# Banded attention and a ratio MLP on one core: where the attention probabilities are transposed

## Chip, cores and metric

One core of one Trainium2 chip runs the whole program. The metric is device time in microseconds, the median of several executions of the same program. Lower is better. The kernel before takes 993.1 us.

## What is computed

The reference is an attention over a causal band of 128 positions, followed by a two-layer MLP whose activation is a ratio of two polynomials:

```python
# batch 8, heads 8, sequence 576, head size 64
scores = scale * q @ k.T + bias           # bias: -slope[head] * distance
mask   = (rel >= 0) & (rel < 128)         # rel = query position - key position
attn   = exp(scores - max); attn = attn / (sum(attn) + 1e-09)
x      = attn @ v                         # as 4608 tokens x 512
h      = x @ w_in                         # 512 x 2048
P = a0 + a1*h + a2*h**2 + a3*h**3
Q = 1 + |b0|*|h| + |b1|*h**2
out    = (P / (Q + 1e-06)) @ w_out        # 2048 x 512
```

## The kernel before

The 4608 tokens are 36 blocks of 128. The MLP works on tiles of two blocks (256 tokens), 18 in all. For each tile, a step takes two chunks of 128 columns of the hidden layer: TensorE makes `h` (24 matmuls of 256 columns, three for each of four slices of the 512 inputs and each chunk, since every f32 factor is split in a high and a low part), the other engines work out the ratio on 128x512 elements, and TensorE adds the chunk to the output sums `acc` (12 matmuls of 512 columns). A tile has 8 steps, the program 144.

The elementwise chain of a step is a line of instructions on three engines, in `mlp`: ScalarE takes |h| (L959) and one linear term (L961), GpSimd makes the denominator (L960, L962), VectorE the numerator (L963, L964), ScalarE takes logarithm and exponential of the denominator (L965, L967), VectorE corrects the reciprocal and multiplies (L968, L969, L975), ScalarE rounds the high part `g_h` (L385), and VectorE subtracts to get the low part `g_l` (L977). `h` lies in a PSUM bank from its first matmul to L977. Three banks (tag `h`) serve `h` and the bank `px` of the attention.

The attention works in units: a pair of heads over two blocks, 76 units, 4 for each later tile. A unit's TensorE work is put into *sessions* between MLP matmuls (`attention`, L667). The session of unit u holds three things, one after the other:

- the transposes of unit u-1's probabilities (`turn_halves`, L593): eight transposes of 64x128 pieces against an identity, written to PSUM, half of them into `px` and half into free columns of the score banks,
- the scores of unit u (`scores`, L537),
- the product of probabilities and values of unit u-2 (`quarters`, L641), into `px` and `py`.

Between the sessions the unit's softmax runs: VectorE moves the upper half of each diagonal block (`copy_predicated`, L561) and adds bias and takes the minimum (L568, the tile `pr`), ScalarE exponentiates and sums (L573), VectorE takes the reciprocal (L584), GpSimd scales `pr` by it (L585, `shares`). After the transposes, ScalarE copies the results out of PSUM into `p_all` (`spread`, L607, three copies by the helper at L385), and GpSimd splits them by two affine selects into the part of the own block and the part of the block before (L619). `quarters` reads `p_all`. After it, `sum_halves` (L652) brings the result into the input `x` of the next tile's MLP.

The order of all instructions on each engine is not written by hand. `Plan.op` records every operation with a due time and a cost for each engine that may do it. `Plan.order` first places a fixed list (`FIRST`, L59), then runs a small model in time in which every free engine takes the ready operation that is due first, and the program is emitted in the order found. So the constants at L355 to L362 (due times) and the costs given to `plan.op` decide the order on every engine.

DMAs are issued by SyncE (SP): the queries, keys and values of a unit (`job`, L477, tiles `kq` and `v`, four buffers each), bias tables (L530) and the output (L1039).

```python
# L681, in attention(u): what a session is made of
emits = [lambda: c.scores(sc)]
if turned: emits.insert(0, lambda: turned.turn_halves(places))
if held:   emits.append(lambda: held["unit"].quarters(...))
```

Of the kernel before, what the change touches and what calls it, by code (L numbers as in the profile page):

```python
# [20 lines left out]
P = 128  # L21
# [318 lines left out]
def banded_attention_ratio_mlp(ctx: ExitStack, tc: tile.TileContext, kqv, w_in, w_out, ab, bias, ident, out):  # L340
# [21 lines left out]
    PAIRED, PA, PT, PD, TO, TL, EO, SO2 = 76, -0.35, 6.0, 3.0, 0.0, 0.1, 0.0, 0.0  # L362
# [145 lines left out]
    class Unit:  # L508

        def __init__(self, u, A):  # L510
            self.u, self.A = u, A
            self.t, self.p, self.j = t, p, j = units[u]
            self.m = m = TILES[j]
            self.n = 2 * m
            self.kinds = [block_type(STARTS[j] + i) for i in range(m)]
            self.blocks = [i for i in range(m) if self.kinds[i] != 1]
            self.kt, self.qt, self.vt, self.kq_keys, self.v_keys = job(u, A)
            self.tables, self.bias_keys = [], []
            for kind in self.kinds:
# [12 lines left out]

# [21 lines left out]
        def softmax(self, sc, heads=(0, 1), lead=0.0):  # L554
# [11 lines left out]
            def top(e, i, h):  # L566
                y = 2 * i + h
                nc.vector.tensor_tensor_reduce(  # L568
                    out=ap(pr)[:, y, :], in0=inside(sc[h])[:, i, Q:], in1=self.tables[i](h), scale=-0.125, scalar=3.0e38,
                    op0=ALU.add, op1=ALU.min, accum_out=ap(st)[:, y : y + 1])  # L570

            def exp(e, y):
                nc.scalar.activation(ap(pr)[:, y, :], ap(pr)[:, y, :], AF.Exp, bias=ap(st)[:, y : y + 1], scale=-1.0, accum_out=ap(st)[:, 4 + y : 5 + y])  # L573

            for i in range(m):
                for h in heads:
                    y = 2 * i + h
                    plan.op(A + 0.6 - lead, {"v": 211}, lambda e, i=i, h=h: top(e, i, h), reads=[(sc[h], 0), self.bias_keys[i]], writes=[(pr, y), (st, y)])
                    plan.op(A + 0.8, {"a": 388}, lambda e, y=y: exp(e, y), reads=[(pr, y), (st, y)], writes=[(pr, y), (st, 4 + y)])

        def shares(self):
# [3 lines left out]
            plan.op(A + 1.2, {"g": 185 + 1.6 * P * n}, lambda e: nc.gpsimd.tensor_tensor(ap(pr)[:, :n], ap(pr)[:, :n], ap(st)[:, 12 : 12 + n, None].to_broadcast([P, n, P]), ALU.mult),  # L585
# [81 lines left out]
    def attention(u):  # L667
# [20 lines left out]
        if held:  # L688
# [3 lines left out]
            writes += [(bank, 0), (held["py"], 0)]  # L692
        o1 = plan.op(A, {"p": cost}, lambda e: [x() for x in emits], reads=reads, writes=writes, rows=0.5)
# [10 lines left out]
        if late:  # L704
# [425 lines left out]
```

## Time and profile before

| | |
|---|---|
| median of 3 runs | 993.1 us (992.41 to 993.13) |
| the profiled execution | 995.22 us, of which 993.5 us are the span from first to last instruction |
| granted TensorE clock | 0.997 of full speed |
| busy: TensorE, VectorE, ScalarE, GpSimd | 99%, 77%, 70%, 55% |
| bytes moved by DMA | 69 MB |

In the profile PE is TensorE, PEld its weight loads, DVE is VectorE, ACT is ScalarE, POOL is GpSimd, SP is SyncE. A line such as L598 is line 598 of the kernel. Times are microseconds unless marked ns.

### The profile page before, as it was taken

The page shows a single profiled execution, that of the slowest core. Times are in us where ns is not written, and L with a number is a line of the kernel's source. Part 1 is how long each engine was busy: PE and PEld are TensorE (multiplying, and loading weights), DVE is VectorE, ACT ScalarE, POOL GpSimd, SP SyncE. Part 2 cuts the span into 40 slices and gives each one's busy share as a digit, 9 for nine tenths or more (in the row PEclk, how much of TensorE's full clock was granted, in tenths as well). Part 3 has the DMA queues.
Part 4 walks back from the last instruction along what each step waited for, and adds up shares of the span by engine and source line. Part 5 has one row for each costly group of instructions (what it writes and reads, how often), then busy time and mean ns, then how long its engine had stood idle before and what let it go on. Part 6 is the DMA issues. An engine that isn't in the chain of part 4 may idle for free.

```text
span 993.5 us, 24565 instructions
## 1 busy us (share of the span) xinstructions
PE 986.2 (99%) x9429; PEld 862.6 (87%) x9431; DVE 769.0 (77%) x1843; ACT 690.6 (70%) x1717; POOL 549.7 (55%) x662
## 2 busy tenths in 40 slices
PE   8999999999999999999999999999999999999998
PEld 5767888888989888898898898988899889898997
DVE  4999988877777877777777877777777777777675
ACT  5999776676767666767667767767666767766563
POOL 3799965555545554545564545455554545454332
PEclk8999999999999999999999999999999999999999
DMA  8973312111212111112111211111111111000000
GB/s 263 342 257 110 105 43 74 44 65 49 71 49 71 44 44 63 56 44 65 54 45 46 74 46 51 66 44 66 53 44 64 55 44 59 37 10 23 1 22 22
DMA packets 45140, 69.08 MB, mean 70 GB/s; under 512 B 4448, under 2 KB 29664, under 8 KB 45024
## 3 DMA queue, kind: packets, MB, share of 16 engines
q1 hardware_dynamic: 44736, 67.26, 20.3%
q8 instruction: 74, 1.21, 0.5%
q14 instruction: 42, 0.34, 0.1%
q10 hardware_dynamic: 288, 0.26, 0.1%
HBM read 58.07 MB, written 9.44 MB: 68 GB/s over the span
## 4 chain that ended last, share of the span: by engine, by line
PE 98%; DMA 1%; SPq 1%; DVE 0%; issue 0%; ACT 0%; ACTq 0%
PE h L931 42%; PE acc L995 42%; PE sc L552 6%; PE px L650 4%; PE px L598 2%; DMA kq<-in_kqv 1%; PE py L650 1%; PE px L742 1%; PE pt L591 0%; PE warm L1051 0%; PE h L937 0%; SPq L486 0%; SPq L844 0%; SPq L487 0%; PE sc L598 0%
## 5 line engine op out<-in xcount | busy, mean ns | idle before, releaser
L931 PE MATMUL h<-x_hi,wi_hi 128*128 128x256 f32 x1024 | 290.9, 284 | 0.0
L931 PE MATMUL h<-x_lo,wi_hi 128*128 128x256 f32 x1024 | 287.9, 281 | 0.0
L931 PE MATMUL h<-x_hi,w_lo 128*128 128x256 f32 x1024 | 287.5, 281 | 0.0
L960 POOL TENSOR_SCALAR g_q<-g_u,babs 128x512 f32<-128x512 f32 x142 | 110.1, 775 | 247.1 <-ACT g_u L959 243.1
L931 PEld LDWEIGHTS h<-x_lo,wi_hi 128*128 128x128 f32 x1024 | 192.6, 188 | 36.3
L995 PE MATMUL acc<-wo_hi,g_h 128*128 128x512 f32 x548 | 220.2, 402 | 0.0
L995 PE MATMUL acc<-w_lo,g_h 128*128 128x512 f32 x548 | 216.3, 395 | 0.0
L931 PEld LDWEIGHTS h<-x_hi,wi_hi 128*128 128x128 f32 x1024 | 193.1, 189 | 23.2 <-issue 1.4
L995 PE MATMUL acc<-wo_hi,g_l 128*128 128x512 f32 x548 | 206.7, 395 | 0.0
L931 PEld LDWEIGHTS h<-x_hi,w_lo 128*128 128x128 f32 x1024 | 193.7, 189 | 0.0
L962 POOL TENSOR_TENSOR g_q<-g_q,g_u 128x512 f32<-128x512 f32 x143 | 185.1, 1295 | 13.8 <-DVE g_q L960 2.9
L965 ACT ACTIVATE g_u<-g_q,guard 128x512 f32<-128x512 f32 x144 | 104.4, 725 | 103.7 <-POOL g_q L962 102.2
L963 DVE TENSOR_TENSOR g_p<-h,g_p 128x512 f32<-128x512 f32 x144 | 99.5, 691 | 90.4 <-ACT g_p L961 88.7
L968 DVE SCALAR_TENSOR_TENSOR g_q<-g_q,h 128x512 f32<-128x512 f32 x144 | 98.7, 685 | 68.3 <-ACT h L967 68.0
L959 ACT ACTIVATE g_u<-h 128x512 f32<-128x512 f32 x141 | 83.9, 595 | 95.8 <-PE h L931 95.7
L619 POOL TENSOR_SCALAR_AFFINE_SELECT p_all<-p_all 128x512 f32<-128x512 f32 (+1 forms) x144 | 90.6, 629 | 69.7 <-ACT p_all L385 61.7
L573 ACT ACTIVATE pr<-pr,st 128x128 f32<-128x128 f32 x288 | 114.7, 403 | 8.1 <-DVE st L568 7.8
L961 ACT ACTIVATE g_p<-h,na 128x512 f32<-128x512 f32 x140 | 108.7, 776 | 0.9 <-PE h L931 0.9
L977 DVE TENSOR_TENSOR g_l<-h,g_h 128x512 fp32r<-128x512 f32 x137 | 93.8, 685 | 19.9 <-ACT g_h L385 19.5
L995 PEld LDWEIGHTS acc<-wo_hi,g_h 128*128 128x128 f32 x548 | 103.2, 188 | 6.2 <-issue 0.7
L964 DVE SCALAR_TENSOR_TENSOR g_p<-g_p,na,h 128x512 f32<-128x512 f32 x144 | 106.8, 742 | 1.8
L969 DVE SCALAR_TENSOR_TENSOR h<-g_p,na,h 128x512 f32<-128x512 f32 x144 | 107.9, 749 | 0.0
(110 smaller groups left out, 1800.2 us busy)
## 6 DMA issues: line engine op xcount, KB each, us to landing
kq<-in_kqv SPq DMA_DIRECT2D x68, 320.0 KB, 3.2
v<-in_kqv SPq DMA_DIRECT2D x68, 192.0 KB, 2.4
out<-o SPq DMA_DIRECT2D x34, 256.0 KB, 2.0
raw_w<-in_w_in SPq DMA_DIRECT2D x16, 512.0 KB, 6.3
raw_w<-in_w_out SPq DMA_DIRECT2D x16, 512.0 KB, 5.2
bias_t<-in_bias SPq DMA_DIRECT2D x44, 64.0 KB, 2.9
kq<-in_kqv SPq DMA_DIRECT2D x4, 192.0 KB, 5.5
kq_first<-in_kqv SPq DMA_DIRECT2D x4, 128.0 KB, 3.0
```

What stands on the lines that cost most here:

```text
L573: nc.scalar.activation(ap(pr)[:, y, :], ap(pr)[:, y, :], AF.Exp, bias=ap(st)[:, y : y + 1], scale=-1.0, accum_out=ap(st)[:, 4 + y : 5 + y])
L931: nc.tensor.matmul(h(i), w[:, k, :], x[:, k, :], start=(k == 0 and m == 0), stop=(k == NKC - 1 and m == len(seq) - 1))
L960: plan.op(E, {"g": tsc, "v": dve(W / 2, 1)} if soon else {"g": tsc}, lambda e: eng[e].tensor_scalar(v(g_q), v(g_u), ap(babs)[:, 1:2], ap(b ...
L961: plan.op(E, either(soon, act(W, 1, 2) - 20, dve(W, 2)), lambda e: nc.scalar.activation(v(g_p), v(h_s), AF.Identity, bias=ap(na)[:, 2:3], ...
L962: plan.op(E, {"g": ttc, "v": dve(W)} if soon else {"g": ttc}, lambda e: eng[e].tensor_tensor(v(g_q), v(g_q), v(g_u), ALU.mult), reads=[(g_ ...
L963: plan.op(E, {"v": dve(W)}, lambda e: nc.vector.tensor_tensor(v(g_p), v(h_s), v(g_p), ALU.mult), reads=[(h_s, 0), (g_p, 0)], writes=[(g_p, ...
L964: plan.op(E, {"v": dve(W, 1)}, lambda e: stt(v(g_p), v(g_p), ap(na)[:, 1:2], v(h_s), ALU.add, ALU.mult), reads=[(h_s, 0), (g_p, 0)], write ...
L965: plan.op(E, {"a": act(W, 0, 1)}, lambda e: nc.scalar.activation(v(g_u), v(g_q), AF.Ln, bias=guard, scale=1.0), reads=[(g_q, 0)], writes=[ ...
L968: plan.op(E, {"v": dve(W)}, lambda e: stt(v(g_q), v(g_q), GUARD, v(h_s), ALU.add, ALU.mult), reads=[(g_q, 0), (h_s, 0)], writes=[(g_q, 0)])
L969: plan.op(E, {"v": dve(W, 1)}, lambda e: stt(v(h_s), v(g_p), ap(na)[:, 0:1], v(h_s), ALU.add, ALU.mult), reads=[(g_p, 0), (h_s, 0)], write ...
L977: plan.op(E, {"v": dve(W)}, lambda e: nc.vector.tensor_tensor(v(g_l), v(h_s), v(g_h).bitcast(F32), ALU.subtract), reads=[(h_s, 0), (g_h, 0 ...
L995: nc.tensor.matmul(ap(accs[n][i]), x[:, sl], w, start=(c == c0 and part == 0 and m == 0), stop=(c == c1 - 1 and (part == 1 or plain) and m ...
```

## The change

From unit 24 to unit 73 (50 units, the four of each tile from the sixth on, without the last two units) the transpose no longer runs on TensorE. VectorE transposes the 16 blocks of 32x32 of each 128x128 matrix where they are, into a tile `z`. `z` is stored to HBM (256 KB), and four loads of 64 KB bring each block to its place in the tile `x_turn`. GpSimd's two affine selects then read `x_turn` in place of `p_all`. For this the columns of `pr` are laid out in four groups of 32 for each of the four matrices, so softmax, scaling and `quarters` address pieces of 32 columns. The three ScalarE copies out of PSUM are gone for these units. `z` and `x_turn` alternate between two buffers each, in memory that earlier parts of the program have left. Some due times of the planner are changed too, and one entry of `FIRST` follows the new numbering.

```diff
-    1294, 1359, 1276, 1369, 1354, 11372, 1319, 1320, 1356, 1373, 1350, 1714, 1376, 1321, 1250, 1322, 1226, 1295, 1297, 1299, 1357, 1277,
+    1294, 1359, 1276, 1369, 1354, 11372, 1319, 1320, 1356, 1373, 1350, 1722, 1376, 1321, 1250, 1322, 1226, 1295, 1297, 1299, 1357, 1277,
...
-    SA, SG, LL, ML, ZA, ME = 0.082, 0, 6.123, 22.844, 0.779, -17.957
+    SA, SG, LL, ML, ZA, ME = 0.082, 0, 6.123, 19.678, 0.779, -17.272
...
-    SL, AW, BL, E0, E1, E2 = -9.614, 22.396, 14.524, 24.893, 13.935, 57.569
+    SL, AW, BL, E0, E1, E2 = -9.614, 22.396, 18.599, 24.893, 13.935, 57.569
...
+    CROSS, CT, CM = 24, 2.27, 0.744
...
+            self.y = (lambda i, h: m * h + i) if self.crossed() else (lambda i, h: 2 * i + h)
...
+        def crossed(self):
+            return CROSS <= self.u < len(units) - 2
...
+        def row(self, y):
+            if not self.crossed():
+                return ap(self.pr)[:, y, :]
+            return ap(self.pr).rearrange("q y c -> q (y c)").rearrange("q (k y c) -> q k y c", y=4, c=32)[:, :, y]
...
+        def cross(self):
+            u, A, m, n, pr = self.u, self.A, self.m, self.n, self.pr
+            z = slot(const, [P, 4, n, 32], F32, "z", tag=("spare0", "part")[u % 2])
+            d = slot(dr4, [P, 4, n, 32], F32, "z_dram")
+            x = slot(const, [P, 4, n, 32], F32, "x_turn", tag=("raw", "w1")[u % 2])
+            w = self.w = slot(sb2, [P, 2, 4 * n, 32], F32, "p_all")
...
+            plan.op(A + CT, {"s": 728}, lambda e: eng[e].dma_start(ap(d), ap(z)), reads=[(z, 0)], writes=[(d, 0)])
+            for k in range(4):
+                r = slice(32 * k, 32 * k + 32)
+                plan.op(A + CT, {"s": 182}, lambda e, k=k, r=r: eng[e].dma_start(ap(x)[r], ap(d)[:, k].rearrange("(g a) y c -> a g (y c)", a=32)), reads=[(d, 0)], writes=[(x, k)])
+            cost = {"g": 135 + 0.93 * n * P}
...
+        if u > CROSS and not turned:
+            cost += 70
...
-        if late:
+        if c.crossed():
+            c.cross()
+        elif late:
             turning.append(c)
```

On TensorE this is one session of the steady part. Before, with the transposes (L598) ahead of the scores (L552) and the value products (L650):

```order
L995 MATMUL acc_8206<-wo_hi,g_l 128x512
L598 MATMUL px<-id_sb,pr 128x64
L598 MATMUL sc_8286<-id_sb,pr 128x64
...
L598 MATMUL px<-id_sb,pr 128x64
L598 MATMUL sc_8291<-id_sb,pr 128x64
L552 MATMUL sc_8286<-kq 64x2x64
L552 MATMUL sc_8291<-kq 64x2x64
...
L650 MATMUL px<-p_all,v 64x128 x2
L650 MATMUL py<-p_all,v 64x128 x2
```

And a session of the change (L558 are the scores, L694 the value products):

```order
L1044 MATMUL acc_8142<-wo_hi,g_l 128x512
L558 MATMUL sc_8421<-kq 64x2x64
L558 MATMUL sc_8423<-kq 64x2x64
...
L694 MATMUL px<-p_all,v 64x128 x2
L694 MATMUL py<-p_all,v 64x128 x2
```

The eight transposes are gone and scores follow the MLP matmul directly; TensorE has 6545 rows where it had 6945. The number of MLP matmuls between sessions changed as well: before, a tile's four sessions stand behind 33 `h` and 14 `acc` matmuls, 39 and 22, 33 and 14, 87 and 46; now behind 48 and 24, 21 and 14, 51 and 22, 72 and 36.

On VectorE the new transpose (L629) stands between the instructions of the MLP's elementwise chain. Before, the chain of one step near there:

```order
L968 SCALAR_TENSOR_TENSOR g_q_8543<-g_q_8543,h_8411 128x512
L969 SCALAR_TENSOR_TENSOR h_8411<-g_p_8541,na_489,h_8411 128x512
L975 SCALAR_TENSOR_TENSOR h_8411<-g_q_8543,h_8411 128x512
L963 TENSOR_TENSOR g_p_8636<-h_8537,g_p_8636 128x512
L977 TENSOR_TENSOR g_l_8644<-h_8411,g_h_8640 128x512
```

Now, in the same part of a step (L1017, L1018, L1024 and L1026 are the old L968, L969, L975 and L977, L1012 the old L963):

```order
L1017 SCALAR_TENSOR_TENSOR g_q_8605<-g_q_8605,h_8481 128x512
L629 STREAM_TRANSPOSE z_8662<-pr_8602 128x512
L1018 SCALAR_TENSOR_TENSOR h_8481<-g_p_8597,na_491,h_8481 128x512
L1012 TENSOR_TENSOR g_p_8668<-h_8583,g_p_8668 128x512
L1024 SCALAR_TENSOR_TENSOR h_8481<-g_q_8605,h_8481 128x512
L1013 SCALAR_TENSOR_TENSOR g_p_8668<-g_p_8668,na_491,h_8583 128x512
L1026 TENSOR_TENSOR g_l_8704<-h_8481,g_h_8697 128x512
```

Of the 50 transposes 11 stand like this one inside a step's last VectorE instructions; 35 stand right behind an L1026, at the end of a step's chain, and of these 10 have the next session's L567 (the old L561) behind them.

On GpSimd the affine selects stood behind the MLP pair (L960, L962) after the session that made the transposes. Before:

```order
L585 TENSOR_TENSOR pr_8371<-pr_8371,st_8372 128x512
L960 TENSOR_SCALAR g_q_8432<-g_u_8423,babs_495 128x512
L962 TENSOR_TENSOR g_q_8432<-g_q_8432,g_u_8423 128x512
L619 AFFINE_SELECT p_all_8489<-p_all_8489 128x4x128 x2
L960 TENSOR_SCALAR g_q_8543<-g_u_8530,babs_495 128x512
```

Now, where `pr_8499` is the scaling of the unit whose selects write `p_all_8701`:

```order
L621 TENSOR_TENSOR pr_8499<-pr_8499,st_8500 128x512
L1009 TENSOR_SCALAR g_q_8605<-g_u_8590,babs_497 128x512
L1011 TENSOR_TENSOR g_q_8605<-g_q_8605,g_u_8590 128x512
L621 TENSOR_TENSOR pr_8602<-pr_8602,st_8603 128x512
L1009 TENSOR_SCALAR g_q_8676<-g_u_8664,babs_497 128x512
L1011 TENSOR_TENSOR g_q_8676<-g_q_8676,g_u_8664 128x512
L636 AFFINE_SELECT p_all_8701<-x_turn_8636 128x512 x2
L1009 TENSOR_SCALAR g_q_8764<-g_u_8760,babs_497 128x512
```

Two MLP pairs and the next unit's scaling now stand between a unit's scaling and its selects.

## Rows read from the trace of the kernel before

**Rows 1.** The page: busy time by engine, and the chain that ended last.

```profile
PE 986.2 (99%) x9429; PEld 862.6 (87%) x9431; DVE 769.0 (77%) x1843; ACT 690.6 (70%) x1717; POOL 549.7 (55%) x662
...
PE 98%; DMA 1%; SPq 1%; DVE 0%; issue 0%; ACT 0%; ACTq 0%
PE h L931 42%; PE acc L995 42%; PE sc L552 6%; PE px L650 4%; PE px L598 2%; DMA kq<-in_kqv 1%; PE py L650 1%; PE px L742 1%; PE pt L591 0%; PE warm L1051 0%; PE h L937 0%; SPq L486 0%; SPq L844 0%; SPq L487 0%; PE sc L598 0%
```

**Rows 2.** All waits of PE: total us, times, longest.

```profile
PE sc L552 <- DMA kq<-in_kqv: 1.4, 1, 1.4
PE warm L1051 <- PEq L1118: 0.8, 1, 0.8
PE px L742 <- POOL p_all L619: 0.5, 2, 0.3
PE warm L1051 <- issue: 0.3, 1, 0.3
```

**Rows 3.** Busy us (count) of PE, PEld, DVE, ACT, POOL; clock, DMA share, GB/s.

```profile
500.00:600.00 100.00, 100.00 (x1019) 89.81 (x1012) 76.32 (x181) 69.68 (x175) 52.26 (x64) 1.00 0.16 53
```

**Rows 4.** Chain that ended last, 505 to 525 us: start, length, what.

```profile
508.71 0.36 PE h L931 x3
509.06 0.46 PE acc L995 x2
...
510.71 0.20 PE px L598
510.92 0.06 PE px L598
...
511.11 0.81 PE sc L552 x18
511.92 0.10 PE px L650
...
512.64 1.13 PE acc L995 x4
...
519.98 0.20 PE px L598
...
520.38 0.81 PE sc L552 x18
```

**Rows 5.** The same view, 57 to 62 us: a session of scores alone.

```profile
59.63 0.82 PE sc L552 x18
```

**Rows 6.** Groups by line and shape: busy us, mean ns of one.

```profile
L962 POOL TENSOR_TENSOR g_q<-g_q,g_u 128x512 f32<-128x512 f32 x143 | 185.1, 1295 | 13.8 <-DVE g_q L960 2.9
L960 POOL TENSOR_SCALAR g_q<-g_u,babs 128x512 f32<-128x512 f32 x142 | 110.1, 775 | 247.1 <-ACT g_u L959 243.1 <-DVE h L969 3.8
L977 DVE TENSOR_TENSOR g_l<-h,g_h 128x512 fp32r<-128x512 f32 x137 | 93.8, 685 | 19.9 <-ACT g_h L385 19.5
L619 POOL TENSOR_SCALAR_AFFINE_SELECT p_all<-p_all 128x512 f32<-128x512 f32 x136 | 87.3, 642 | 67.1 <-ACT p_all L385 60.6 <-DVE o L1036 1.9
L385 ACT COPY p_all<-sc 128x128 f32<-128x128 f32 x120 | 29.2, 274 | 7.6 <-DVE sc L561 3.7 <-DVE st L568 0.5 <-PE sc L552 0.5
L385 ACT COPY p_all<-px 128x256 f32<-128x256 f32 x62 | 23.5, 379 | 3.3 <-PE py L650 1.9
```

**Rows 7.** Timeline of all engines, 512.9 to 513.7 us.

```profile
512.42 0.68 DVE L977 TENSOR_TENSOR g_l<-h,g_h 128x512 fp32r<-128x512 f32 x1
...
512.73 0.33 SPq L496 DMA_DIRECT2D v<-in_kqv  x1
...
513.61 0.28 PE L931 MATMUL h<-x_hi,wi_hi 128*128 128x256 f32 x1
```

**Rows 8.** Timeline of POOL, 505 to 532 us: start, length, instruction.

```profile
517.75 1.04 POOL L585 TENSOR_TENSOR pr<-pr,st 128x512 f32<-128x512 f32 x1 [0.72 <-DVE st L584]
...
528.95 1.04 POOL L585 TENSOR_TENSOR pr<-pr,st 128x512 f32<-128x512 f32 x1 [0.30 <-DVE st L584]
```

**Rows 9.** DMA issues: KB each, median us from issue to landing.

```profile
out<-o SPq DMA_DIRECT2D x34, 256.0 KB, 2.0
...
bias_t<-in_bias SPq DMA_DIRECT2D x44, 64.0 KB, 2.9
...
v<-in_kqv SPq DMA_DIRECT2D x4, 128.0 KB, 6.0
```

More of the change, by code (lines that the diff above doesn't have):

```diff
@@ L566, in top @@
             def top(e, i, h):
-                y = 2 * i + h
+                y = self.y(i, h)
                 nc.vector.tensor_tensor_reduce(
-                    out=ap(pr)[:, y, :], in0=inside(sc[h])[:, i, Q:], in1=self.tables[i](h), scale=-0.125, scalar=3.0e38,
+                    out=self.row(y), in0=self.like(inside(sc[h])[:, i, Q:]), in1=self.like(self.tables[i](h)), scale=-0.125, scalar=3.0e38,
                     op0=ALU.add, op1=ALU.min, accum_out=ap(st)[:, y : y + 1])
             def exp(e, y):
-                nc.scalar.activation(ap(pr)[:, y, :], ap(pr)[:, y, :], AF.Exp, bias=ap(st)[:, y : y + 1], scale=-1.0, accum_out=ap(st)[:, 4 + y : 5 + y])
+                nc.scalar.activation(self.row(y), self.row(y), AF.Exp, bias=ap(st)[:, y : y + 1], scale=-1.0, accum_out=ap(st)[:, 4 + y : 5 + y])
             for i in range(m):
                 for h in heads:
-                    y = 2 * i + h
+                    y = self.y(i, h)
                     plan.op(A + 0.6 - lead, {"v": 211}, lambda e, i=i, h=h: top(e, i, h), reads=[(sc[h], 0), self.bias_keys[i]], writes=[(pr, y), (st, y)])
@@ L584, in shares @@
             plan.op(A + 1, {"v": 100}, lambda e: nc.vector.reciprocal(ap(st)[:, 12 : 12 + n], ap(st)[:, 8 : 8 + n]), reads=[(st, 8)], writes=[(st, 12)])
[L585 removed]
+            plan.op(A + 1.2, {"g": 185 + 1.6 * P * n}, lambda e: self.scale(),
                     reads=[(pr, y) for y in range(n)] + [(st, 12)], writes=[(pr, y) for y in range(n)])
@@ new lines, in cross @@
+        def cross(self):
[4 more added lines that the diff above has]
+            w = self.w = slot(sb2, [P, 2, 4 * n, 32], F32, "p_all")
+            plan.op(A + CT, {"v": 69 + 1.042 * n * P}, lambda e: nc.vector.transpose(ap(z).rearrange("q k y c -> q (k y c)"), ap(pr).rearrange("q y c -> q (y c)")), reads=[(pr, y) for y in range(n)], writes=[(z, 0)], follows=([*(y[0] for y in heads.values())], [parts[1]])[u % 2] if u < CROSS + 2 else (), sb=True)
+            plan.op(A + CT, {"s": 728}, lambda e: eng[e].dma_start(ap(d), ap(z)), reads=[(z, 0)], writes=[(d, 0)])
[3 more added lines that the diff above has]
+            cost = {"g": 135 + 0.93 * n * P}
+            for k, sign in ((1, 1), (0, -1)):
+                plan.op(A + CM - 0.1 * k, cost, lambda e, k=k, sign=sign: nc.gpsimd.affine_select(
+                    out=ap(w)[:, k].rearrange("q (g y) c -> q g y c", g=4), in_=ap(x), pattern=[[32 * sign, 4], [0, n], [sign, 32]], compare_op=ALU.is_ge, fill=0.0, base=k - 1, channel_multiplier=-sign), reads=[(x, j) for j in range(4)], writes=[(w, k)])
@@ L639, in into, with share @@
             return ap(x)[:, self.p, b0 : b0 + self.m * P]
+        def share(self, r, h, i, own, q0, q1):
+            if not self.crossed():
+                return ap(self.w)[r, h, 2 * i + own, q0:q1]
+            return ap(self.w)[r, own].rearrange("q (g y) c -> q g y c", g=4)[:, q0 // 32 : q1 // 32, self.m * h + i]
         def quarters(self, first, second):
@@ L649, in quarters @@
                             d = slice(64 * h, 64 * h + 64)
-                            nc.tensor.matmul((second if half else first)(i)[d, q0:q1], self.vt(i + own)[r, d], ap(self.w)[r, h, 2 * i + own, q0:q1], start=n == 0, stop=n == len(seen[0]) - 1, tile_position=(Q * half, 64 * h))
+                            nc.tensor.matmul((second if half else first)(i)[d, q0:q1], self.vt(i + own)[r, d], self.share(r, h, i, own, q0, q1), start=n == 0, stop=n == len(seen[0]) - 1, tile_position=(Q * half, 64 * h))
         def sum_halves(self, at, bank, col, others):
```

16 lines of the change are left out of this document (14 added, 2 removed).

## Prediction

> **What bounds the kernel now.** I read the page first: TensorE is busy 99% of the span and the chain that ended last is 98% TensorE [rows 1]. Busy time alone would not prove it, since matmuls overlap, so I then asked what TensorE ever waited for: four kinds of wait, 3.0 us in 993.5 [rows 2], and in a stretch of the steady part TensorE is busy 100 of 100 us [rows 3]. So in the steady part every microsecond of TensorE's line of work is a microsecond of the kernel, and no other engine makes it late. The chain in order of time shows what that line consists of [rows 4]: three `h` matmuls take 0.36 us, two `acc` matmuls 0.46, and a session is a block of 1.93 us (510.71 to 512.64) in which the transposes (L598) run from 510.71 to 511.11, then the scores 0.81, then the value products 0.72. The first four `acc` matmuls behind a session take 1.13 in place of 0.92, so leaving it costs 0.2.
>
> **What is removed.** The transposes of 50 units. In the chain one session's transposes last 511.11 - 510.71 = 0.40 us, and in the next session 520.38 - 519.98 = 0.40 [rows 4]; the page agrees, since 2% of 993.5 over 62 such sessions is about 0.3 to 0.4 each [rows 1]. Does the whole 0.40 go? Its first piece is 0.20 where the others are 0.06, so up to 0.14 of it could be the cost of entering a session, which would then fall on the scores. The session of scores without transposes answers: its scores take 0.82 [rows 5] against 0.81 behind transposes [rows 4]. So entering is not passed on, and I take 0.40: 50 x 0.40 = **20.0 us** off the path.
>
> Here a rule speaks against the change. The Trainium skill, "VectorE: DVE Perf Modes", section "Rules for kernel authors", says to transpose 128x128 on TensorE whenever a PSUM destination will do. Its section "The three transpose paths" prices such a transpose at 390 ns (bf16, alone); by that figure an estimate for the four of a unit is 1.56 us, 78 us for 50 units, and the sum would be 915. The trace does not agree: eight halves run in pairs and cost 0.40 together, and the row decides.
>
> Also removed are three ScalarE copies a unit, 2 x 274 + 379 = 927 ns [rows 6]. They lie beside TensorE's work, which does not wait for them, so I count no gain.
>
> **What is added on VectorE.** 50 transposes of 128x512 f32. The trace shows none. The nearest row is L977, 0.69 us, also 128x512 f32 to memory outside PSUM [rows 6]; I take that, and half and double of it (0.3 and 1.4) as ends. 50 x 0.69 = 34 us go on an engine that is busy 76 of 100 us in the steady part [rows 3], so VectorE comes to about 81% and does not become the bound by its sum. But it works in order, and the order puts 11 of the 50 inside the last instructions of a step's chain. What that chain holds is a PSUM bank: before, a step's L977 ended at 513.10 and TensorE began the next `h` at 513.61 [rows 7], 0.5 us to spare at one of the tighter places. A chain that is 0.69 later would make TensorE wait 0.2 there; at 11 places 2.1 us, if all were that tight. The ends are 0 and, with 1.4 for the transpose, 11 x 0.9 = 10; I take half of 2.1, **1.0 us**, since not all are.
>
> **What is added on the way to the value products.** Store, four loads, two selects. None costs TensorE anything if `p_all` is there in time, so the question is the slack. A unit's scores begin at session u and its values at session u+2, 0.81 behind that session's start. With 0.12 per `h` and 0.23 per `acc` [rows 4] and a session of 1.93 + 0.20 - 0.40 = 1.73, the new gaps are 7.5 us (21 and 14), 12.9 (51 and 22), 13.0 (48 and 24) and 18.7 (72 and 36). The shortest two in a row make 20.4, so the tightest units, two of four in each tile, have 20.4 + 0.8 = **21.2 us**. The way, taken at its longest: scaling ends 7.7 to 9.6 us after the scores' start (518.79 - 511.11, 529.99 - 520.38) [rows 4, 8], so 9.6; an instruction ahead on VectorE and the transpose, 0.69 each; the store, as large as the output's, 2.0 [rows 9]; four loads, each as large as a bias table, 2.9 [rows 9] behind three issues of 0.33 [rows 7], 3.9; an MLP pair ahead on GpSimd, 0.78 + 1.30 = 2.1, and two selects of 0.64 [rows 6], 1.3. Together **20.3 us**: it fits with 0.9 to spare, so I count 0. The selects move on GpSimd from behind one MLP pair to behind two, and at the head of its queue they would hold the next pair; by the same sum they are ready in time.
>
> On SP the store waits for VectorE and the first load for the store, and a load of `kq` or `v` can stand behind either. Such a load is issued as soon as a session frees a buffer (512.73, right behind the session that ended at 512.64) [rows 4, 7], and is wanted two sessions later, 20 us away; a hold of some us costs nothing. The bytes grow by 50 x 512 KB, 26 MB on 69, on DMA engines that are 16% busy [rows 3].
>
> **What changes without being counted.** The value products now read pieces of 32 columns in place of rows of 128. The trace has no such read on TensorE. The ends are 0 and a doubling, 50 x 0.72 = 36 us [rows 4]. I take 0, as nothing makes it likely that contiguous runs of 32 stream slower. Strided pieces on ScalarE, VectorE and GpSimd (`pr` in four parts) are covered by the slack above.
>
> **Sum.** -20.0 + 1.0 = -19.0. For the profiled execution 995.2 - 19.0 = 976.2, its span 974.5. The median of the runs is 2.1 lower than that execution, and I predict against the median: 993.1 - 19.0 = **974.1 us**.
>
> **Rivals.**
> - *Entering the session is passed on.* 0.14 of each 0.40 stays: 50 x 0.26 = 13.0, and 993.1 - 13.0 + 1.0 = 981.1. For it: the first piece of 0.20. Against it: the 0.82 [rows 5], which is one session early in the program. 12%.
> - *VectorE is held at its head.* Of the transposes 10 stand ahead of the next session's first softmax instruction. In the gap of 7.5 its scores end 8.3 after the unit's own, while scaling may end at 9.6; with the transpose, VectorE comes to it at 10.3, 2.0 late, and the MLP chain behind it as well. Less the 0.5 to spare this is 1.5 a tile, in 12.5 tiles 19 us: the gain is gone, 993. Against it: only if the step behind is really waiting then. 6%.
> - *Slower: the round trip through HBM comes late.* TensorE then waits at L694 in the two tight units of each tile, 25 in all. If the loads land in 6.0 us, as the 128 KB ones of the start did [rows 9], the way is 3.1 longer, 2.2 late, 55 us: 974 + 55 = 1029. It decides from where 25 sessions lose 20 us, 0.8 each: loads that land in 2.9 + 0.9 + 0.8 = 4.6. For it: five DMAs in two dependent stages where there were none. Against it: those 6.0 us come from the crowded start, while the 2.9 us are the median of 44 loads of the same size. The Trainium skill, "VectorE: DVE Perf Modes", section "The three transpose paths", warns of this side: a plain DMA that transposes by strides is 19 times slower than the crossbar's. It means large strides in the innermost direction, while here each piece is 512 bytes in one run; no run here shows the slow form. 6%.
> - *Slower: pieces of 32 columns stream at half speed.* 993.1 - 19.0 + 36 = 1010. 4%.
>
> **How the numbers follow.** The forecast has 72%, the rivals 12, 6, 6 and 4. What a measurement can tell from no change is about 0.2%, 2 us. Faster are the forecast, the first rival and a third of the second: 86%; the same, half of the second: 3%; slower the rest: 11%. The range goes down to 970, since 0.40 is read from pieces rounded to 0.01 and each 0.05 of it is 2.5 us, and up to 985, which takes in the first rival and most of the 10 us that a transpose of 1.4 would cost. It leaves out the last three rivals, 16%.
>
> **What would show it.** In the profile after: no L598 behind the first third, and in the chain the scores directly behind an MLP matmul with 0.81 still; the chain still 98% TensorE. Waits of TensorE in the steady part: none or a few tenths at `h` <- VectorE (the 1.0). A wait at L694 for L636 would show the round trip late, and the landing times of `z_dram` and `x_turn` say by how much. Value products longer than 0.72 a session would show the reads of 32 columns; scores of 0.95 the first rival; waits of VectorE at L629 the second. The forecast is wrong if TensorE's waits come to more than some 10 us.

## The result: 981.9 us, 11.2 faster, and the profile after

| | before | changed |
|---|---|---|
| median (lowest to highest) | 993.12 us (992.41 to 993.29) | 981.92 us (981.46 to 982.46) |
| ratio, 95% interval | | 0.9889 [0.9872, 0.9906] |
| the profiled execution, its span | 995.22, 993.5 | 981.46, 979.7 |
| busy: TensorE, VectorE, ScalarE, GpSimd | 99%, 77%, 70%, 55% | 99%, 82%, 68%, 56% |
| bytes moved by DMA | 69 MB | 95 MB |

Faster as forecast and inside the range, but by 11.2 us where 19.0 were worked out. (The two profiled spans lie 13.8 apart, since in that of before the same `h` matmul comes 2.5 us later already at 231 us, ahead of the changed sessions; the medians are compared.) In the changed kernel the lines are numbered anew: `h` L931 is L980, `acc` L995 is L1044, the chain of a step L959 to L977 is L1008 to L1026, scores L552 are L558, value products L650 are L694, the mask copy of the softmax L561 is L567, scaling L585 is L621, ScalarE's copies and casts L385 are L387. New are VectorE's transpose L629, the store and loads L630 and L633, and the selects L636.

The page after, busy time and the chain that ended last:

```profile
PE 971.1 (99%) x9029; PEld 840.7 (86%) x9031; DVE 806.6 (82%) x1929; ACT 666.8 (68%) x1567; POOL 549.3 (56%) x626
...
PE 87%; DVE 5%; DMA 3%; ACT 2%; issue 1%; SPq 1%; POOL 0%; ACTq 0%; DVEq 0%
PE h L980 39%; PE acc L1044 39%; PE sc L558 4%; PE px L694 3%; DMA raw_w<-in_w_in 2%; DMA kq<-in_kqv 1%; DVE g_p L1012 1%; DVE g_l L1026 1%; ACT g_p L1010 1%; DVE h L1018 1%; DMA raw_w<-in_w_out 1%; PE py L694 1%; DVE w L906 0%; ACT g_u L1008 0%; DVE g_q L1017 0%
```

Against [rows 1] the transposes L598 are gone from the chain, and TensorE's share of it falls from 98% to 87%: L1012, L1026, L1010 and L1008, instructions of a step's chain, now stand in it. The prediction had it stay at 98%. The waits of PE say where they come in:

```profile
PE h L980 <- DVE g_l L1026: 2.3, 10, 0.4
...
PE px L791 <- POOL p_all L658: 0.5, 2, 0.3
```

The first line is new against [rows 2]: TensorE stands at the first `h` matmul of a step until VectorE has made `g_l` of an earlier step, that is, until the PSUM bank is handed back. The view names 10 waits and 2.3 us. It counts only time in which the engine shows as idle, and the last `acc` matmuls, which overlap, hide a part. So I also measured from the start of one matmul to the start of the next: an `h` that follows an `acc` starts 0.23 us after it. Between 200 and 900 us no such pair of before is more than 0.05 longer; in the changed kernel 24 are, by 5.8 us together: nine of 0.36 to 0.39, one of 0.57, the others 0.07 to 0.23. The first `h` behind such a wait also holds TensorE 0.08 longer (the next `h` starts 0.19 behind it, not 0.12), 24 x 0.08 = 1.9. Together 7.7 us.

That is most of what is missing. I compare a stretch of 44 sessions (11 tiles) by the starts of the sessions: 285.68 to 872.35 before, 286.20 to 863.28 after, 586.67 and 577.08 us. From its first matmul to the MLP matmul behind it a full session took 1.93 us and takes 1.54, 0.39 less, so 44 x 0.39 = 17.2 us were to be won, 9.6 came, 7.6 are missing. Of the 24 waits 21 lie in this stretch, 5.2 + 21 x 0.08 = 6.9 us of the 7.6; the rest is in spacings that are each less than 0.05 longer. All parts of the sessions themselves came as forecast. The chain after:

```profile
535.39 0.81 PE sc L558 x18
...
536.93 1.14 PE acc L1044 x4
```

Scores 0.81 and four `acc` in 1.14, as in [rows 4]; between them the value products take 536.93 - 536.20 = 0.73, where they took 0.72. The work that was moved, by groups and by DMA issues:

```profile
L636 POOL TENSOR_SCALAR_AFFINE_SELECT p_all<-x_turn 128x512 f32<-128x512 f32 x100 | 70.3, 727 | 7.0 <-DMA x_turn<-z_dram 7.0
...
L629 DVE STREAM_TRANSPOSE z<-pr 128x512 f32<-128x512 f32 x50 | 35.6, 711 | 7.6 <-POOL pr L621 7.4
```

```profile
z_dram<-z SPq DMA_DIRECT2D x50, 256.0 KB, 2.0
x_turn<-z_dram SPq DMA_DIRECT2D x200, 64.0 KB, 2.0
```

VectorE's transpose takes 0.71 us, against the 0.69 taken from [rows 6], the store lands in 2.0 and a load in 2.0 (2.9 was taken from [rows 9]); GpSimd waits for the loads 7.0 us in all and TensorE never at L694.

**The turn that became too short.** The next two fences are the timelines of the two kernels around a session of the same kind (columns: start, length, engine, line). Before; the L977 that starts at 512.42 and the `h` at 513.61 stand in [rows 7]:

```profile
510.51 0.60 ACT L959 ACTIVATE g_u<-h 128x512 f32<-128x512 f32 x1 [1.77 <-PE h L931]
...
511.81 0.69 DVE L963 TENSOR_TENSOR g_p<-h,g_p 128x512 f32<-128x512 f32 x1 [0.95 <-ACT g_p L961]
...
513.67 0.42 DVE L561 COPY_PREDICATED sc<-id_sb,sc 128x256 f32<-128x256 uint32 x1
```

And after:

```profile
516.18 0.60 ACT L1008 ACTIVATE g_u<-h 128x512 f32<-128x512 f32 x1 [0.82 <-PE h L980]
...
517.48 0.69 DVE L1012 TENSOR_TENSOR g_p<-h,g_p 128x512 f32<-128x512 f32 x1
...
518.09 0.42 DVE L567 COPY_PREDICATED sc<-id_sb,sc 128x256 f32<-128x256 uint32 x1
...
518.42 0.68 DVE L1026 TENSOR_TENSOR g_l<-h,g_h 128x512 fp32r<-128x512 f32 x1
...
519.25 0.36 PE L980 MATMUL h<-x_hi,wi_hi 128*128 128x256 f32 x1 [0.19 <-DVE g_l L1026]
```

A session stands between two steps' `h`. When the `h` ahead of it is ready, ScalarE starts on it (L959, L1008), and VectorE's order has that step's L963 or L1012 ahead of the L977 or L1026 that hands back the bank of the step before. So a piece of chain runs beside the session and begins where the session begins. Before, it lasts 513.10 - 510.51 = 2.59 us, and TensorE comes to the next `h` at 513.61 [rows 7], 3.10 after the same start. After, the chain lasts 519.10 - 516.18 = 2.92, because the mask copy L567, which stood behind L977 before, is now ahead of L1026 and takes 0.33; TensorE follows L1026's end by 0.15. TensorE's own way is 3.10 - 0.40 = 2.70. So it waits 2.92 + 0.15 - 2.70 = 0.37 us, and 0.36 is what it shows. Two things made that wait, the shorter session and the place of L567. In VectorE's order the mask copy is directly ahead of the bank's last instruction at 4 places before, none later than 259 us, and at 23 after, 21 of them among the 50 units, from 274 us on. It stands so at 20 of the 24 waits; the other four, of 0.14 to 0.19, have the shorter session alone.

### The profile page after: what moved, and what is told of

Read it like the earlier page. It is cut to its first block, busy times and chain, and to the rows that moved or that the text cites. A ratio compares the mean times of both kernels' runs of the same rounds, so it can differ in the third digit from the quotient of the medians.

```text
span 979.7 us, 24224 instructions
## 1 busy us (share of the span) xinstructions
PE 971.1 (99%) x9029; PEld 840.7 (86%) x9031; DVE 806.6 (82%) x1929; ACT 666.8 (68%) x1567; POOL 549.3 (56%) x626
## 4 chain that ended last, share of the span: by engine, by line
PE 87%; DVE 5%; DMA 3%; ACT 2%; issue 1%; SPq 1%; POOL 0%; ACTq 0%; DVEq 0%
PE h L980 39%; PE acc L1044 39%; PE sc L558 4%; PE px L694 3%; DMA raw_w<-in_w_in 2%; DMA kq<-in_kqv 1%; DVE g_p L1012 1%; DVE g_l L1026 1%; ACT g_p L1010 1%; DVE h L1018 1%; DMA raw_w<-in_w_out 1%; PE py L694 1%; DVE w L906 0%; ACT g_u L1008 0%; DVE g_q L1017 0%
## 5 line engine op out<-in xcount | busy, mean ns | idle before, releaser
L980 PE MATMUL h<-x_hi,wi_hi 128*128 128x256 f32 x1024 | 291.9, 285 | 2.4 <-DVE g_l L1026 2.3
L980 PE MATMUL h<-x_lo,wi_hi 128*128 128x256 f32 x1024 | 287.6, 281 | 0.0
L980 PE MATMUL h<-x_hi,w_lo 128*128 128x256 f32 x1024 | 287.3, 281 | 0.0
L1009 POOL TENSOR_SCALAR g_q<-g_u,babs 128x512 f32<-128x512 f32 x142 | 109.4, 770 | 216.9 <-ACT g_u L1008 211.8
L980 PEld LDWEIGHTS h<-x_lo,wi_hi 128*128 128x128 f32 x1024 | 192.6, 188 | 35.2
L1044 PE MATMUL acc<-wo_hi,g_h 128*128 128x512 f32 x548 | 221.8, 405 | 0.0
L980 PEld LDWEIGHTS h<-x_hi,wi_hi 128*128 128x128 f32 x1024 | 192.9, 188 | 33.4 <-issue 14.0
L1044 PE MATMUL acc<-w_lo,g_h 128*128 128x512 f32 x548 | 216.2, 395 | 0.0
L1044 PE MATMUL acc<-wo_hi,g_l 128*128 128x512 f32 x548 | 208.6, 395 | 0.0
L980 PEld LDWEIGHTS h<-x_hi,w_lo 128*128 128x128 f32 x1024 | 193.6, 189 | 0.0
L1011 POOL TENSOR_TENSOR g_q<-g_q,g_u 128x512 f32<-128x512 f32 x143 | 184.8, 1293 | 13.9 <-DVE g_q L1009 2.9
L1017 DVE SCALAR_TENSOR_TENSOR g_q<-g_q,h 128x512 f32<-128x512 f32 x144 | 98.5, 684 | 77.0 <-ACT h L1016 75.1
L1008 ACT ACTIVATE g_u<-h 128x512 f32<-128x512 f32 x141 | 84.2, 597 | 82.0 <-PE h L980 81.9
L621 POOL TENSOR_TENSOR pr<-pr,st 128x512 f32<-128x512 f32 (+1 forms) x76 | 75.7, 996 | 107.9 <-DVE st L590 32.4
L387 ACT CAST g_h<-h 128x512 fp32r<-128x512 f32 x134 | 78.6, 586 | 69.1 <-DVE h L1024 62.7
L1012 DVE TENSOR_TENSOR g_p<-h,g_p 128x512 f32<-128x512 f32 x144 | 98.7, 685 | 30.7 <-ACT g_p L1010 30.2
L1044 PEld LDWEIGHTS acc<-wo_hi,g_h 128*128 128x128 f32 x548 | 103.1, 188 | 7.8 <-issue 1.2
L1026 DVE TENSOR_TENSOR g_l<-h,g_h 128x512 fp32r<-128x512 f32 x137 | 94.0, 686 | 17.8 <-ACT g_h L387 16.3
L1010 ACT ACTIVATE g_p<-h,na 128x512 f32<-128x512 f32 x140 | 108.6, 776 | 0.0
```

What stands on the lines that cost most here:

```text
L980: nc.tensor.matmul(h(i), w[:, k, :], x[:, k, :], start=(k == 0 and m == 0), stop=(k == NKC - 1 and m == len(seq) - 1))
L1008: plan.op(E, either(soon, act(W, 1), dve(W)), lambda e: nc.scalar.activation(v(g_u), v(h_s), AF.Abs) if e == "a" else nc.vector.tensor_sca ...
L1009: plan.op(E, {"g": tsc, "v": dve(W / 2, 1)} if soon else {"g": tsc}, lambda e: eng[e].tensor_scalar(v(g_q), v(g_u), ap(babs)[:, 1:2], ap(b ...
L1010: plan.op(E, either(soon, act(W, 1, 2) - 20, dve(W, 2)), lambda e: nc.scalar.activation(v(g_p), v(h_s), AF.Identity, bias=ap(na)[:, 2:3], ...
L1011: plan.op(E, {"g": ttc, "v": dve(W)} if soon else {"g": ttc}, lambda e: eng[e].tensor_tensor(v(g_q), v(g_q), v(g_u), ALU.mult), reads=[(g_ ...
L1012: plan.op(E, {"v": dve(W)}, lambda e: nc.vector.tensor_tensor(v(g_p), v(h_s), v(g_p), ALU.mult), reads=[(h_s, 0), (g_p, 0)], writes=[(g_p, ...
```

## Experiments

I came to that reading only by the end of the runs. At first there were three theories for the 8 us: A, VectorE's transposes make L1026 late (the prediction's reason for its 1.0); B, the new order itself, the way in which sessions and steps are placed; C, the round trip holds GpSimd's queue and with it the chain. All runs, with the length of the 44 sessions and the waits at `h` behind `acc` between 200 and 900 us (number, sum), both read from the timeline of PE as above:

| kernel | median, us | ratio to before, 95% | 44 sessions | waits at `h` |
|---|---|---|---|---|
| before | 993.1 | | 586.7 | 0 |
| changed | 981.92 | 0.9889 [0.9872, 0.9906] | 577.1 | 24, 5.8 |
| no transposes on VectorE | 982.49 | 0.9894 [0.9878, 0.9910] | 576.9 | 23, 5.5 |
| transposes run twice | 983.30 | 0.9897 [0.9876, 0.9918] | 577.9 | 26, 6.1 |
| no round trip | 983.29 | 0.9899 [0.9886, 0.9913] | 576.8 | 24, 5.7 |
| before, new due times | 993.15 | 1.0002 [0.9992, 1.0012] | 587.4 | 2, 1.1 |
| changed, old due times | 985.70 | 0.9933 [0.9920, 0.9945] | 581.3 | 22, 10.8 |
| bank freed sooner, everywhere | 980.67 | 0.9876 [0.9862, 0.9889] | 571.9 | 0 |
| bank freed sooner, from pass 6 | 977.74 | 0.9848 [0.9835, 0.9860] | 572.9 | 0 |
| the same, and the planner told | 987.29 | 0.9941 [0.9929, 0.9953] | 583.6 | 12, 9.7 |
| before, bank freed sooner | 992.87 | 0.9998 [0.9989, 1.0006] | 586.8 | 0 |
| sessions padded | 993.60 | 0.9997 [0.9987, 1.0008] | 586.1 | 7, 1.5 |
| mask copy behind L1026 | 977.94 | 0.9842 [0.9829, 0.9856] | 573.9 | 15, 2.3 |
| mask copy behind, bank sooner | 978.00 | 0.9852 [0.9838, 0.9865] | 573.3 | 0 |

### No transposes on VectorE

```diff
-  plan.op(A + CT, {"v": 69 + 1.042 * n * P}, lambda e: nc.vector.transpose(...z, ...pr), ...)
-  plan.op(A + CT, {"s": 728}, lambda e: eng[e].dma_start(ap(d), ap(z)), ...)
+  plan.op(A + CT, {"v": 69 + 1.042 * n * P}, lambda e: None, ...)
+  plan.op(A + CT, {"s": 728}, lambda e: eng[e].dma_start(ap(d), ap(pr)...), ...)
```

> The changed kernel (981.9 us) with the 50 VectorE transposes left out: the store reads the scaled probabilities directly, so the probabilities reach the value products without the transpose inside the blocks. All other instructions and their order stay. Theory A (the 34 us of transposes delay the last VectorE instruction of a step, which holds a PSUM bank that TensorE waits for): TensorE's waits for L1026 go, 975 to 977 us. Theory B (the new order alone puts the next h too close behind the old one, whatever VectorE does): 981 to 982 us. Theory C (the round trip through HBM holds GpSimd's queue): 981 to 982 us.

982.49 us, and the same waits at the same places. Theory A falls: VectorE's 35.6 us of transposes cost the kernel nothing, and they do not make L1026 late.

### Transposes run twice

The other direction, run later: each L629 twice, so that VectorE goes from 806.6 to 833.4 us busy.

```diff
-  lambda e: nc.vector.transpose(ap(z)..., ap(pr)...)
+  lambda e: [nc.vector.transpose(ap(z)..., ap(pr)...) for _ in range(2)]
```

> The changed kernel with VectorE's transpose run twice for each of the 50 units: 36 us more of VectorE's work (50 x 0.711), which takes it from 82% to 86%. If VectorE has room (leaving the transposes out gave nothing), 981 to 984 us. If VectorE is at its limit wherever the chain of a step waits on it, each doubling delays that chain by up to 0.7 us: 985 to 1015 us with longer waits at h.

983.3, at the upper edge of the room expected of the first theory, with 0.8 us more in the 44 sessions. VectorE has room for this much again.

### No round trip

The store and the four loads are left out and the selects read `z`, so every block stays at its untransposed place in the matrix.

```diff
-  plan.op(A + CT, {"s": 728}, lambda e: eng[e].dma_start(ap(d), ap(z)), ...)
+  plan.op(A + CT, {"s": 728}, lambda e: None, ...)
...
-  plan.op(A + CT, {"s": 182}, lambda e, k=k, r=r: eng[e].dma_start(ap(x)[r], ...), ...)
+  plan.op(A + CT, {"s": 182}, lambda e, k=k, r=r: None, ...)
...
-  in_=ap(x), pattern=[[32 * sign, 4], ...
+  in_=ap(z), pattern=[[32 * sign, 4], ...
```

> The changed kernel without the round trip: no store and no loads, the affine selects read the blocks that VectorE transposed where they lie, so blocks are not at their place. All other instructions and their order stay. Theory A and theory B: 981 to 982 us, since TensorE never waits for the selects. Theory C: GpSimd's 7 us of waits for the loads go and with them most of what TensorE lost, 975 to 977 us.

983.29, again the same waits. That is 1.3 above the upper end of what theories A and B gave; the 44 sessions take 576.8, as in the changed kernel, and in the profiled execution they begin 0.8 later, so most of the excess lies ahead of them; it is not explained. Theory C falls, and the zero that the prediction gave the round trip holds: taking it away wins nothing.

### Due times apart from the crossing

The kernel before with the new due times alone:

```diff
-    SA, SG, LL, ML, ZA, ME = 0.082, 0, 6.123, 22.844, 0.779, -17.957
+    SA, SG, LL, ML, ZA, ME = 0.082, 0, 6.123, 19.678, 0.779, -17.272
...
-    SL, AW, BL, E0, E1, E2 = -9.614, 22.396, 14.524, 24.893, 13.935, 57.569
+    SL, AW, BL, E0, E1, E2 = -9.614, 22.396, 18.599, 24.893, 13.935, 57.569
...
-    PAIRED, PA, PT, PD, TO, TL, EO, SO2 = 76, -0.35, 6.0, 3.0, 0.0, 0.1, 0.0, 0.0
+    PAIRED, PA, PT, PD, TO, TL, EO, SO2 = 76, 0.021, 6.0, 3.0, 2.141, -0.573, -0.55, 0.883
```

> The kernel before (993.1 us) with the due times of the changed kernel and nothing else. Theory A: the order by itself costs little, 992.5 to 994.5 us. Theory B: the due times that the change brings are what makes banks turn late, so this is slower than before by 3 to 7 us, 996 to 1000 us.

993.15: the due times cost nothing while the sessions are long. Nor does the place of the mask copy by itself: this kernel has it directly ahead of L977 at 10 places from 309 us on, and neither of its two waits is at one of them. The reverse, the changed kernel with these three lines as they were before, tells the rest:

> The changed kernel (VectorE's transposes and the way by HBM) with the due times ML, ME, BL, PA, TO, TL, EO and SO2 of the kernel before, so that the planner lays out another order. If the waits at h come from the shorter session against a chain of fixed length: waits at h between 4 and 10 us again, 980 to 988 us. If they come from the changed due times with the crossing: no waits at h beyond the 1.65 us of the kernel before, 974 to 977 us.

985.7 with 22 waits, most of 0.37 and the longest 1.61:

```profile
PE h L980 <- DVE g_l L1026: 7.2, 22, 1.4
```

At each of the 22 the mask copy stands directly ahead of L1026. So the waits come with the short session, under either set of due times, and the new set makes them smaller. Theory B, that the order alone does it, does not hold in that form.

### The bank handed back sooner

L1024 writes its result to `g_p` in SBUF, not over `h`, and the cast and L1026 read it there. The bank is free when L1024 ends. The planner is not told, so no instruction moves. Here for all passes, with the calls shortened:

```diff
-  stt(v(h_s), v(g_q), 2.0, v(h_s), ALU.subtract, ALU.mult)          # L1024
+  stt(v(g_p), v(g_q), 2.0, v(h_s), ALU.subtract, ALU.mult)
-  copy(e, v(g_h), v(h_s))                                           # the cast
+  copy(e, v(g_h), v(g_p))
-  nc.vector.tensor_tensor(v(g_l), v(h_s), v(g_h), ALU.subtract)     # L1026
+  nc.vector.tensor_tensor(v(g_l), v(g_p), v(g_h), ALU.subtract)
```

> The changed kernel in the same order, but L1024 writes its product to an SBUF tile instead of back into the PSUM bank of h, and the cast and L1026 read that tile: the bank of h is free at the end of L1024, about 1.5 us sooner. Nothing is left out. Theory A and theory B (both say TensorE loses its time waiting for a bank of h): the waits go, 974 to 977 us. Theory C: 981 to 982 us. If reading SBUF makes the cast and L1026 slower, the chain to the acc matmuls grows by at most 0.2 us a step, which has slack.

980.67, above the 974 to 977 that was expected. The waits at `h` are gone and the 44 sessions are 5.2 us shorter; but the part ahead of them became 3.3 longer (a session there starts at 237.20, not at 233.89), so only 1.9 shows between the profiled spans and 1.3 between the medians. The next run keeps the edit to passes 6 and later, the steady part:

```diff
+  g_r = g_p if n >= 6 else h_s
```

(`g_r` in the place of `g_p` in the lines above.)

> Bank theory: PE's waits at h come from the bank of h, which is read until L1026; an earlier kernel that freed it 1.5 us sooner everywhere lost 3 to 4 us before step 32 and took back 6 us after it. Here the same is done only from pass 6 (step 32) on, and the order on all engines is unchanged; the early stretch is then as in the changed kernel. Expected 975 to 977 us, ratio to before 0.982 to 0.984, no waits at h for g_l, excess spacing from acc to h below 2 us. Rival (the new order costs the 8 us somewhere else, and takes back what is removed at the bank): within 1 us of the changed kernel's 981.9.

977.74, 4.2 below the changed kernel: the bank is the place. It is 0.7 above the upper end of what was expected. The groups of this kernel, by line and shape, show what it pays:

```profile
L1026 DVE TENSOR_TENSOR g_l<-g_p,g_h 128x512 fp32r<-128x512 f32 x112 | 121.7, 1086 | 19.8 <-ACT g_h L387 19.1
...
L1009 POOL TENSOR_SCALAR g_q<-g_u,babs 128x512 f32<-128x512 f32 x142 | 117.5, 828 | 169.6 <-ACT g_u L1008 165.5 <-DVE h L1018 3.8
...
L636 POOL TENSOR_SCALAR_AFFINE_SELECT p_all<-x_turn 128x512 f32<-128x512 f32 x100 | 82.2, 845 | 19.3 <-DMA x_turn<-z_dram 18.7 <-issue 0.3
...
L1026 DVE TENSOR_TENSOR g_l<-h,g_h 128x512 fp32r<-128x512 f32 x25 | 17.1, 685 | 1.6 <-ACT g_h L387 1.3
```

The 112 L1026 with both inputs in SBUF take 1.09 us where the 25 with one in PSUM take 0.69, and GpSimd's L1009 and L636 rise from 0.77 and 0.73 to 0.83 and 0.85, while its L1011 stays (1.29 and 1.30). That VectorE is 28 us busier fits the worse early part of the run before, and 5 waits of 0.37 at `acc` matmuls (ScalarE's copy of the sums is late) are new; that the one follows from the other is argued, not shown.

The control, the same edit in the kernel before:

> The kernel before with the same edit of the bank from pass 6 on and nothing else. Bank theory: its PE does not wait at h, so nothing is to be had: 992.5 to 993.5 us, ratio 0.999 to 1.001. Rival (the edit by itself makes VectorE's or ScalarE's work shorter and would help any kernel): 986 to 990 us.

992.87. Where TensorE does not wait for the bank, freeing it sooner is worth nothing. And the edit with the planner told of it, so that it lays out an order of its own:

> The same as the kernel that frees the bank sooner from pass 6 on, but the planner is told of it, so that it makes its own order, all engines' rows move. Bank theory: no more wait at h after acc either; the order may be better or worse in other places, so 973 to 980 us. Rival (order, not bank): the planner's new order is what counts, and the excess at h after acc stays above 4 us.

A miss: 987.3.

```profile
PE h L980 <- DVE g_p L1024: 12.3, 18, 1.0
```

The planner's model now sees the bank free at L1024 and uses that room up; TensorE waits at L1024 longer than it did at L1026. That the model's errors of some tenths are what TensorE then waits for is a reading of this, not tested.

### Sessions made long again

Half of a unit's scores are computed a second time in each of the 50 sessions; the planner's costs stay, so nothing else moves.

```diff
-        def scores(self, sc):
-            for i in range(self.m):
+        def scores(self, sc, again=False):
+            for i in range(1 if again else self.m):
...
+            emits.insert(0, lambda: c.scores(sc, True))    # if u > CROSS and not turned
```

> The changed kernel with each of the 50 sessions that lost its transposes made longer again: half of the unit's score matmuls are run twice, about 0.41 us (half of the 0.82 us that a session of scores alone took), and the planner's costs are left alone, so that nothing else moves. If the waits at h come from the missing time between a step's chain and its turn at the bank (the shorter session), the padding costs 20.5 us of TensorE's time but takes the 6.6 us of waits away: 981.9 + 20.5 - 6.6 = 996 us, with an excess from acc to h of about 1.7 us. If they come from the new order itself, they stay: 1002 us and an excess of 8.

The session became 0.33 longer (1.54 to 1.87), not 0.41, so 50 x 0.33 = 16.5 us were added; the time rose by 11.7. In the 44 sessions 14.5 were added and 9.1 show. The rest is waits that went: their sum falls from 5.8 to 1.5. Of the 7 left four are of 0.05; the other three, 0.27 to 0.55, are at places that had none before the padding, and were not looked into. The same turn as above (lines behind the inserted one are numbered one higher, so L1009, L1027 and L981 are L1008, L1026 and L980):

```profile
521.87 0.60 ACT L1009 ACTIVATE g_u<-h 128x512 f32<-128x512 f32 x1 [0.81 <-PE h L981]
...
523.77 0.42 DVE L567 COPY_PREDICATED sc<-id_sb,sc 128x256 f32<-128x256 uint32 x1
...
524.10 0.68 DVE L1027 TENSOR_TENSOR g_l<-h,g_h 128x512 fp32r<-128x512 f32 x1
...
524.93 0.35 PE L981 MATMUL h<-x_hi,wi_hi 128*128 128x256 f32 x1
```

The chain is as long as before the padding, 524.78 - 521.87 = 2.91, with the mask copy ahead as it was, and TensorE begins `h` at 524.93, 0.15 after the chain's end. The turn's sum says the same: 2.92 + 0.15 - (2.70 + 0.33) = 0.04. Of each 0.33 us of work added to a session, 0.10 had been a wait before.

### The mask copy behind L1026

The other half of the cause. After the planner has made its order, L567 changes places with L1026 wherever it is directly ahead of it in VectorE's order. (There are 21 such places; the 14 in the expectation were counted in a shortened list.)

```diff
     order = plan.order()
+    on_v = [i for i, o in enumerate(order) if o.engine == "v"]
+    for i, j in zip(on_v, on_v[1:]):
+        if order[i].part == "mask" and order[j].part == "low":
+            order.insert(j, order.pop(i))
```

> The changed kernel with one swap at 14 places of VectorE's order: the mask copy of the scores (L567) behind the L1026 that hands the bank back, not ahead of it; no other instruction moves. Theory of two causes: before, TensorE had 0.51 us between L977's end and its next h, of which 0.14 is the handing over, so 0.37 to spare; the session is 0.40 shorter and L567 takes 0.33 ahead of L1026, which makes the wait of 0.36 seen. Without L567 it is 0.03: about 4.5 to 5 of the 5.8 us of waits go, 976.5 to 977.5 us, ratio to before 0.983 to 0.984. Rival (the shorter session alone does it, the mask copy is beside the path): the waits stay, 981 to 983 us. Other rival: the softmax that begins 0.69 later makes something else late, and the time is above 978 without waits at h.

977.94, 4.0 below the changed kernel, with nothing else moved. The timeline at the same turn:

```profile
514.71 0.60 ACT L1008 ACTIVATE g_u<-h 128x512 f32<-128x512 f32 x1 [0.82 <-PE h L980]
...
516.01 0.69 DVE L1012 TENSOR_TENSOR g_p<-h,g_p 128x512 f32<-128x512 f32 x1
...
516.11 0.59 ACT L387 CAST g_h<-h 128x512 fp32r<-128x512 f32 x1
...
516.73 0.69 DVE L1026 TENSOR_TENSOR g_l<-h,g_h 128x512 fp32r<-128x512 f32 x1
...
517.34 0.42 DVE L567 COPY_PREDICATED sc<-id_sb,sc 128x256 f32<-128x256 uint32 x1
...
517.57 0.35 PE L980 MATMUL h<-x_hi,wi_hi 128*128 128x256 f32 x1
```

The chain is 517.42 - 514.71 = 2.71, and the wait 2.71 + 0.15 - 2.70 = 0.16; of the nine waits near 0.36 eight became 0.12 to 0.16 and one went, as did those of about 0.12; the one of 0.57 became 0.40, and the four that had no mask copy ahead of L1026 stayed, 0.14 to 0.19. It did not fall to 0.03, because L1026 now waits for ScalarE's cast, which ends at 516.70; the cast itself starts at 516.11, right behind VectorE's L1024 (515.38 to 516.07), which writes what it reads. Taken with the padded run, both causes are shown: either the copy's 0.33 or the session's 0.33 given back removes 3.5 to 4.3 of the 5.8 us. Both ways of freeing the bank at once:

> The swap of the 14 places together with the bank that is freed sooner from pass 6 on. If both take away the same waits, the second adds nothing: 976.5 to 978 us, like the better of the two alone. If they take away different things, the gains add: below 975 us.

978.0, no better than either alone: they take away the same waits. The versions with the mask copy behind L1026 and with the bank freed sooner from pass 6 are equally fast within their intervals, and both beat the changed kernel.

## Why the prediction was right in sign and 8 us off in size

- **The 20.0 us of transposes: right.** A session went from 1.93 to 1.54 us, 0.39 each, 19.5 in all. The rival that entering a session is passed on to the scores falls: they take 0.81 still, and the spacing from an `acc` matmul to the session is 0.32 in both.
- **"I take half of 2.1, 1.0 us", the bank turn: this is the step that failed.** The place was right (`h` waits for L977, now L1026, and the chain of the profile shows it), the size was not: 7.7 us in 24 waits, not 1.0. It stands inside the ends of 0 and 10, whose upper end came from a transpose of 1.4 us, a reason that was also wrong. So it is partly luck that 981.9 lies in the range: its room up to 985 was made for such a transpose and for the first rival, and neither came. Three things were missed in "0.5 us to spare". 0.15 of it is the handing over from VectorE to TensorE. The change itself takes 0.40 off the other side, because the session that it shortens is the time in which that chain runs: the 0.40 was counted as gained and not as taken from the spare. And the scores are ready sooner, so the mask copy, 0.33, comes ahead of L1026 in VectorE's order; the prediction looked in that order for transposes and not for what else had moved. 0.36 - 0.40 - 0.33 gives the wait of 0.37.
- **The reason given for the 1.0, transposes inside the chain: wrong.** Left out or run twice, they move the waits by about 0.3 us at most.
- **0 for the round trip: right**, with more room than the sum had (loads land in 2.0, not 2.9), and no wait at L694. The rival of 1029 us had no ground.
- **0 for pieces of 32 columns: right**, 0.73 against 0.72.
- **VectorE at about 81%: right** (82.80 of 100 us in the window of [rows 3]), and the rival that it is held at its head falls with the doubled transposes.

The windows of 100 us show how little one sees of all this in a share:

```profile
500.00:600.00 100.00, 99.58 (x950) 88.45 (x949) 82.80 (x201) 66.38 (x158) 53.30 (x58) 1.00 0.28 93
```

TensorE is at 99.58, where it was at 100.00.

The rule of the Trainium skill that the prediction set against the change ("VectorE: DVE Perf Modes", section "Rules for kernel authors": transpose 128x128 on TensorE where a PSUM destination will do) does not decide this kernel: here TensorE was the bound and gave 0.39 us a unit, while VectorE's 0.71 cost nothing. (The estimate of 915 that the prediction gave by that page leaves out its own 1.0; with it the sum is 916.)

Open: counted at the same `h` matmul of both kernels, the distance in the profiles grows from 2.5 us at 231 us to 13.6 at the end, 11.1 of the 19.5; the 24 waits are 7.7 of the 8.4 that are missing, and the other 0.7 was not looked into. The last 0.14 of each wait was not tried either: since the cast stands right behind L1024, it would take a VectorE chain that brings L1024 sooner, as far as this turn shows.

## What to carry to other kernels

Work that is removed from the engine that bounds the kernel is also time in which the others were catching up. Before counting it as won, find the piece of chain that runs beside it and must end before that engine's next use of a buffer with the least to spare, subtract the removed time from its spare, and read in the new order which instructions now stand ahead of its last one. Here most of such a wait was mended by the place of one short instruction, 4.0 us; the planner, only told of more room, laid out an order that was 5.4 slower than the changed kernel.

## What was not expected of the hardware

A VectorE instruction on 128x512 f32 with two inputs in SBUF took 1.09 us on average (median 1.12, from 0.68 to 1.55) where the same one with an input in PSUM takes 0.69, and two of GpSimd's instructions rose at the same time, by 0.06 and 0.12. The Trainium skill, "SBUF — State Buffer", section "SBUF: two separate sides", says that VectorE and GpSimd share a pair of ports, which a VectorE instruction with two SBUF inputs and a GpSimd instruction that reads SBUF take exclusively, the later one waiting. The times agree in direction: the shortest is that of the undisturbed form, the 12 of the 112 that overlap GpSimd's work by less than 0.1 us take 0.69 on average and the other 100 take 1.13, and GpSimd is busy 59% of that run. So moving an operand out of PSUM to free a bank has a price of its own, 0.40 us an instruction here; in the kernel before with the same edit it is 0.57 (1.25 on average), and the time stays the same (992.87).

The 200 loads that put the blocks in place, 64 KB in pieces of 512 bytes, land in 2.0 us, as the 256 KB store does; on DMA engines that are 28% busy in the steady part, 26 MB of traffic cost the kernel nothing.
